# Linear attention and a soft mixture of experts on one core: joined early loads, a split weight load, and a first output chunk whose odd rows are stored in uneven pieces

## The chip, the core and the metric

The kernel runs on one core of one Trainium2 chip. A core has a tensor engine (PE, with its weight loads PEld), a vector engine (DVE), a scalar engine (ACT), GpSimd (POOL) and SyncE (SP), which work in parallel and wait for one another on semaphores, and sixteen DMA engines that move data between the chip's memory (DRAM) and the core's SBUF. The metric is the device time of one execution in microseconds. The profile is one more execution, recorded; its span runs from the first to the last recorded instruction.

## What is computed

The reference makes linear attention over 64 heads, joins the heads to 4608 tokens of 512 numbers, and sends the tokens through a soft mixture of 8 experts. All numbers are float32.

```python
def _attn_ref(q, k, v, g_norm):
    kv = np.einsum('bhsd,bhse->bhde', k, v)
    out = np.einsum('bhsd,bhde->bhse', q, kv)
    rms = np.sqrt(np.mean(out * out, axis=-1, keepdims=True) + 1e-06)
    return (out / rms * g_norm).astype(np.float32)

def _moe_ref(x, phi, w1, w2):
    logits = x @ phi
    d = np.exp(logits - logits.max(0, keepdims=True))
    d /= d.sum(0, keepdims=True) + 1e-09
    slot_input = (d.T @ x).reshape(E, S_per_e, D)
    for e in range(E):
        slot_out[e] = np.maximum(slot_input[e] @ w1[e], 0.0) @ w2[e]
    c = np.exp(logits - logits.max(1, keepdims=True))
    c /= c.sum(1, keepdims=True) + 1e-09
    return (c @ slot_out.reshape(n_slots, D)).astype(np.float32)
```

Here q, k and v are 8 x 8 x 576 x 64, phi is 512 x 32 (8 experts of 4 slots), each w1 is 512 x 1024 and each w2 is 1024 x 512. Inputs and result together are 71 MB.

## The kernel before

**Memory.** Nearly all of SBUF is one buffer, `arena`, in blocks of 256 columns; `place(at, n)` is n columns from block `at`. `KV_AT` and `Q_AT` say where the keys and values of each of the 8 batches (`kv`) and the queries of each pair of batches (`q`) lie, `W_AT` where the weights go that later overwrite them, `OUT_AT` where the 12 chunks of the result are put. A load or a store is one DMA instruction of 128 rows, one for each partition of SBUF, so that each of the sixteen DMA engines has 8 rows of it.

**Loads.** All DMAs are issued by SP, one after the other, each when its place is free. The first eight stand ahead of everything: `first` (constants and the first half of the first kv block), the second half of that block, the main part of the first q block, the second kv block in two halves, the rest of the first q block, the third kv block, the main part of the second q block. Three more follow once the first kv block is used up. The others wait for a tile of the main loop (`loads_behind`): the last kv and q blocks at tile 9, weights at tiles 18, 24 and 27. `W_ROWS` lists which weights share a load: its fourth row holds half of w2 of expert unit 2, w1 of expert 6 and w1 of expert 5, and is loaded after the last tile.

**Main loop.** 36 tiles of 128 tokens, T = 0 to 35. For each tile PE multiplies queries with a block-diagonal matrix `bd` made from k and v (`products`), ACT squares and copies the result out of PSUM (`square`, `evict`), DVE sums squares and logits, POOL scales rows (`scale_x`, `scale_part`). The matrix of a batch b is made in three steps: step 0 and step 1 multiply keys with values, step 2 (`slots`) transposes and fills `bd`. `kv_steps` says after which tile's turn a step stands: entry (b, i) is i tiles from the batch's first tile, `first[b]` = 9 * (b // 2) + 4 * (b % 2). A step stands ahead of `products` of its tile.

**Experts and output.** After the loop come the sums over the slots, `expert_h` (first matrix), `expert_y` (second matrix, in two halves hf of the result's columns), then `gather` and `mix`, and `output(hf, k, f)` for each of the 12 chunks: n = 0 to 5 for the first half, 6 to 11 for the second. A chunk is 1536 columns of `arena`. `OUT_ROWS` says which chunks go out in one store: chunks 0 to 2, 3 to 5, 6 and 7, 8 to 11; the store is issued once the last chunk of its row stands in `arena`. Between the chunks PE still multiplies for the second half: `expert_y(2, 1)` to `expert_y(5, 1)` after chunk 3, `expert_y(6, 1)` and `expert_y(7, 1)` after chunk 5. Their weights come with the last two loads (`load_w("w2", 5)`, `load_w("w2", 7)`).

**Order and waits.** The class `Order` records every instruction and derives the waits from what is read and written. All instructions therefore carry the line of its `emit`, L204 before and L208 after. At the end SP waits for those DMAs that nobody else waited for.

Of the kernel before, what the change touches and what calls it, by code (L numbers as in the profile page):

```python
# [5 lines left out]
F32 = mybir.dt.float32  # L6
# [5 lines left out]
P = 128  # L12
# [15 lines left out]
TOK = 4608  # L28
# [4 lines left out]
KV_AT = (0, 36, 54, 0, 90, 126, 18, 54)  # L33
Q_AT = (18, 72, 108, 36)
# [8 lines left out]
    (("w1", 4, None), ("w2", 2, 1), ("w2", 0, None), ("w2", 1, None)),  # L43
    (("w2", 2, 0), ("w1", 6, None), ("w1", 5, None)),
    (("w1", 7, None),),
# [4 lines left out]
OUT_AT = (32, 38, 44, 104, 110, 116, 122, 128, 134, 140, 146, 152)  # L50
OUT_ROWS = ((0, 1, 2), (3, 4, 5), (6, 7), (8, 9, 10, 11))
SHARED = (5, 11)
HEAD = 144
# [210 lines left out]

def soft_moe_linear_attention(nc, first_in, kv_in, q0_in, q1_in, kv4_in, kv5_in, t3_in, w_in, out):


    const = Const(nc)
# [12 lines left out]
    def load_row(at, src):  # L281
        nc.sync.dma_start(place(at, src.shape[-1]), src)
# [30 lines left out]
    def w_block(kind, u, i):  # L313
# [6 lines left out]
    nc.sync.dma_start(arena[:, : HEAD + 2304], first_in)  # L320
    load_row(KV_AT[0] + 9, kv_in[0, :, 2304:])
    load_row(Q_AT[0], q0_in[:, :2048])
    load_row(KV_AT[1], kv_in[1, :, :2304])
    load_row(KV_AT[1] + 9, kv_in[1, :, 2304:])
    load_row(Q_AT[0] + 8, q0_in[:, 2048:])
    load_row(KV_AT[2], kv_in[2])
    load_row(Q_AT[1], q1_in)

# [4 lines left out]
        24: lambda: load_w("w1", 2),  # L333
        27: lambda: load_w("w1", 4),
    }

# [6 lines left out]
    zeros = const.tile([P, 256], BF16, name="zeros")  # L343
    nc.vector.memset(zeros, 0.0)
    eps = const.tile([P, 1], F32, name="eps")
    nc.gpsimd.memset(eps, EPS_RMS)
# [6 lines left out]
    for i in range(2):  # L353
        lo = 64 * i
# [268 lines left out]
    first = {b: 9 * (b // 2) + 4 * (b % 2) for b in range(B)}  # L623
    kvs = {}
    kv_steps = {(b, i - 3): (i,) for b in range(2, B) for i in range(3)}
    kv_steps.update({(1, -2): (0,), (1, -1): (1, 2)})
    kv_steps.update({(6, i - 4): (i,) for i in range(3)})
# [49 lines left out]
    for g in range(2):  # L677
# [6 lines left out]
        fill(EARLY[1 + g], cols=512)  # L684
    load_row(KV_AT[3], kv_in[3])
    load_row(Q_AT[1] + 8, kv4_in)
    load_row(Q_AT[2], kv5_in)
    T_at, diag_at, pb_at, d_at, sums_at = {}, {}, {}, {}, {}
    for T in range(NT - 2):
# [3 lines left out]
        o = products(T)  # L693
# [182 lines left out]
    def mix(hf):  # L876
# [3 lines left out]
        zs[hf] = halves(f"z{hf}", pz)  # L880

    def output(hf, k, f):
        z = zs[hf]
# [4 lines left out]
        for v in range(2):  # L888
# [21 lines left out]
            else:  # L910
                nc.vector.tensor_copy(out=st[:, 2:4], in_=pots[0][:, :, : CT * NS])
        for row in OUT_ROWS:
            if row[-1] == n:
                lo, m = row[0] * 4 * CT * NS, len(row) * 4 * CT * NS
                nc.sync.dma_start(
                    out[:, lo * P : (lo + m) * P].rearrange("o (p n) -> (o p) n", p=P), place(OUT_AT[row[0]], m)
                )

    expert_h(0)
    expert_h(1)  # L920
# [42 lines left out]
def build_program():  # L963
    import concourse.bacc as bacc

    nc = bacc.Bacc("TRN2", target_bir_lowering=False, num_devices=1, dynamic_dma_scratch_size=SCRATCH)
    shapes = {
        "first": (P, HEAD + 2304), "kv": (4, P, TOK), "q0": (P, TOK), "q1": (P, 2048),
        "kv4": (P, 2560 + TOK), "kv5": (P, 2 * TOK), "t3": (P, 3 * TOK),
        "w": (1, 2 * NE * P * UNIT),  # L970
    }
    args = [nc.dram_tensor(f"in_{n}_dram", s, F32, kind="ExternalInput").ap() for n, s in shapes.items()]
    args.append(nc.dram_tensor("out_0_dram", (1, 4 * NCH * P * 4 * CT * NS), F32, kind="ExternalOutput").ap())
    order = Order(nc)
    soft_moe_linear_attention(order, *args)
    order.emit()
    return nc
# [58 lines left out]
```

## Time and profile before

| | us |
|---|---|
| median of 3 runs (172.42 to 172.51) | 172.49 |
| the profiled execution | 172.53 |
| its span | 171.2 |
| PE busy (87% of the span) | 149.1 |
| ACT busy (52%) | 88.9 |
| DVE busy (50%) | 86.0 |
| POOL busy (33%) | 57.2 |

DMA engines moved 71.67 MB in 3476 packets, 419 GB/s on the mean over the span. Matmuls overlap one another, so PE's share is not a measure of its reserve. A wait is read from the idle time just ahead of an instruction and from what ended it. A DMA is seen at three points: when SP issues it, when its rows are moved, and when the last of them has landed.

### The profile page before, as it was taken

The page shows a single profiled execution, that of the slowest core. Times are in us where ns is not written, and L with a number is a line of the kernel's source. Part 1 is how long each engine was busy: PE and PEld are TensorE (multiplying, and loading weights), DVE is VectorE, ACT ScalarE, POOL GpSimd, SP SyncE. Part 2 cuts the span into 40 slices and gives each one's busy share as a digit, 9 for nine tenths or more (in the row PEclk, how much of TensorE's full clock was granted, in tenths as well). Part 3 has the DMA queues.
Part 4 walks back from the last instruction along what each step waited for, and adds up shares of the span by engine and source line. Part 5 has one row for each costly group of instructions (what it writes and reads, how often), then busy time and mean ns, then how long its engine had stood idle before and what let it go on. Part 6 is the DMA issues. An engine that isn't in the chain of part 4 may idle for free.

```text
span 171.2 us, 4497 instructions
## 1 busy us (share of the span) xinstructions
PE 149.1 (87%) x1975; PEld 108.1 (63%) x1975; DVE 86.0 (50%) x184; ACT 88.9 (52%) x230; POOL 57.2 (33%) x68
## 2 busy tenths in 40 slices
PE   7787897989999899999899999999999988989400
PEld 3467776979688888898797775455565444445100
DVE  1122156283677265763936798724897027137400
ACT  2037576786965887768849864203213025137400
POOL 6000708548356755466482579200000000000000
PEclk9999999999999999999999999999999999999965
DMA  5999999999999999999999999998999999999995
GB/s 192 416 422 433 439 415 437 472 421 474 417 413 458 430 426 430 406 404 452 433 492 419 431 429 389 434 450 354 436 478 387 461 390 421 439 396 439 406 459 241
DMA packets 3476, 71.67 MB, mean 419 GB/s; under 512 B 384, under 2 KB 384, under 8 KB 384
## 3 DMA queue, kind: packets, MB, share of 16 engines
q1 hardware_dynamic: 3456, 71.38, 97.6%
q8 instruction: 15, 0.25, 0.5%
q14 instruction: 5, 0.04, 0.1%
HBM read 61.94 MB, written 9.44 MB: 417 GB/s over the span
## 4 chain that ended last, share of the span: by engine, by line
PE 47%; DMA 26%; ACT 12%; DVE 5%; SPq 2%; issue 1%
PE psum L204 47%; DMA arena<-in_kv_dram 13%; DMA arena<-in_w_dram 13%; ACT bd L204 3%; ACT sq L204 3%; ACT xall L204 2%; SPq L204 2%; DVE logits L204 1%; ACT arena L204 1%; DVE ms L204 1%; ACT part L204 1%; ACT d L204 1%; ACT r L204 1%; DVE r L204 0%; DVE d L204 0%
## 5 line engine op out<-in xcount | busy, mean ns | idle before, releaser
L204 PE MATMUL psum<-bd,arena 128*128 128x192 f32 (+1 forms) x320 | 56.1, 335 | 1.9 <-ACT bd L204 1.5
L204 PEld LDWEIGHTS psum<-bd,arena 128*128 128x128 f32 (+1 forms) x320 | 45.4, 179 | 7.1 <-ACT bd L204 2.8
L204 DVE TENSOR_REDUCE ms<-sq 128x16 f32<-128x1024 f32 (+1 forms) x19 | 22.1, 1162 | 32.6 <-ACT sq L204 32.3
L204 POOL TENSOR_TENSOR xall<-xall,r 128x512 f32<-128x512 f32 x34 | 34.8, 1044 | 0.0
L204 POOL TENSOR_TENSOR part<-part,r 128x512 f32<-128x512 f32 x17 | 17.8, 1049 | 49.7 <-DVE r L204 49.7
L204 ACT ACTIVATE sq<-psum 128x512 f32<-128x512 f32 x36 | 21.5, 598 | 12.6 <-PE psum L204 12.4
L204 PE MATMUL psum<-arena 128*64 128x64 f32 (+1 forms) x640 | 21.7, 226 | 3.3 <-DMA arena<-in_kv_dram 2.2
L204 PEld LDWEIGHTS psum<-arena 128*64 128x64 f32 (+1 forms) x640 | 19.0, 137 | 7.9 <-DMA arena<-in_kv_dram 3.5
L204 ACT COPY xall<-psum 128x512 f32<-128x512 f32 x34 | 20.6, 606 | 0.0
L204 ACT COPY part<-psum 128x256 f32<-128x256 f32 (+1 forms) x38 | 13.6, 359 | 9.9 <-DVE part L204 8.8
L204 DVE TENSOR_REDUCE logits<-part 128x64 f32<-128x512 f32 (+1 forms) x18 | 17.8, 991 | 0.0
L204 PE MATMUL psum<-arena,xall 128*32 128x256 f32 x256 | 15.0, 380 | 0.4 <-DMA arena<-in_w_dram 0.2
L204 DVE COPY arena<-psum 128x768 f32<-128x768 f32 (+1 forms) x12 | 10.4, 889 | 8.4 <-PE psum L204 8.4
L204 ACT COPY arena<-psum 128x768 f32<-128x768 f32 (+1 forms) x14 | 10.1, 755 | 8.3 <-PE psum L204 8.3
L204 PE MATMUL psum<-logits,part 32*128 32x384 f32 x96 | 12.8, 521 | 1.5 <-ACT arena L204 0.9
L204 PE MATMUL psum<-arena,sq 128*32 128x256 f32 x224 | 12.7, 379 | 0.2 <-DVE sq L204 0.2
L204 PEld LDWEIGHTS psum<-arena,xall 128*32 128x32 f32 x256 | 8.0, 110 | 7.3 <-DMA arena<-in_w_dram 1.8
L204 PE MATMUL psum<-xall,d 128*32 128x129 f32 x288 | 10.8, 278 | 0.9 <-ACT d L204 0.9
L204 ACT COPY bd<-psum 64x128 f32<-64x128 f32 (+1 forms) x32 | 9.9, 309 | 1.6 <-PE psum L204 1.4
L204 PEld LDWEIGHTS psum<-logits,part 32*128 32x128 f32 x96 | 6.1, 183 | 7.1 <-ACT arena L204 4.2
L204 PEld LDWEIGHTS psum<-arena,sq 128*32 128x32 f32 x224 | 7.2, 110 | 5.2 <-DVE sq L204 0.6
L204 PEld LDWEIGHTS psum<-xall,d 128*32 128x32 f32 x288 | 7.0, 109 | 4.1 <-ACT d L204 2.2
(74 smaller groups left out, 118.9 us busy)
## 6 DMA issues: line engine op xcount, KB each, us to landing
arena<-in_w_dram SPq DMA_DIRECT2D x4, 4096.0 KB, 19.9
arena<-in_w_dram SPq DMA_DIRECT2D x1, 7168.0 KB, 27.5
arena<-in_t_dram SPq DMA_DIRECT2D x1, 6912.0 KB, 36.1
arena<-in_w_dram SPq DMA_DIRECT2D x1, 5120.0 KB, 17.9
arena<-in_kv_dram SPq DMA_DIRECT2D x2, 2304.0 KB, 23.4
arena<-in_kv_dram SPq DMA_DIRECT2D x1, 4608.0 KB, 42.6
out_dram<-arena SPq DMA_DIRECT2D x2, 2304.0 KB, 9.6
arena<-in_kv_dram SPq DMA_DIRECT2D x1, 3584.0 KB, 32.2
```

Of the source, the lines that this page charges most:

```text
L204: inst = getattr(engine, method)(*args, **kwargs)
```

## The change

There are four edits.

1. **Joined early loads.** The second half of the first kv block and the main part of the first q block become one load, `kq0` (4352 columns); the two halves of the second kv block become one, `kv1`; the third kv block and the main part of the second q block become one, `kq2` (6656 columns). Eight early loads become five.
2. **Order of kv steps.** Batch 1 has steps 0, 1 and 2 all ahead of tile 3 (before: step 0 ahead of tile 2, steps 1 and 2 ahead of tile 3). Batch 2 has steps 0 and 1 ahead of tile 7 and step 2 ahead of tile 8 (before: one step each ahead of tiles 6, 7 and 8).
3. **Split w1 load.** w1 of expert 5 leaves its row of `W_ROWS` and is loaded behind tile 30; half of w2 unit 2 and w1 of expert 6 stay where the whole row was.
4. **First store.** Chunks 0 to 2 are no longer stored by one DMA of 128 rows. As soon as chunk 0 is there, its 64 odd rows (6,144 bytes each) go out in four pieces, `APART`: 26 rows as 2 x 13 from POOL, 11 rows as 2 x 11 half rows from POOL, 15 rows as 5 x 3 and 12 rows as 3 x 4 from SP. Once chunk 2 is there, the even rows of all three chunks (64 rows of 18,432 bytes) and the odd rows of chunks 1 and 2 (64 rows of 12,288 bytes) go out from SP. Two small loads on POOL into a new tile `steps`, with 7 and 6 outer pieces, stand ahead of POOL's first and second store. The host puts the pieces back in order.

```diff
     (("w1", 4, None), ("w2", 2, 1), ("w2", 0, None), ("w2", 1, None)),
-    (("w2", 2, 0), ("w1", 6, None), ("w1", 5, None)),
+    (("w1", 5, None),),
+    (("w2", 2, 0), ("w1", 6, None)),
...
+CHUNK = 4 * 12 * 32
+APART = (("gpsimd", 0, 26, 2, 1), ("gpsimd", 41, 11, 2, 2), ("sync", 26, 15, 5, 1), ("sync", 52, 12, 3, 1))
+STEPS = (7, 6)
...
-    load_row(KV_AT[0] + 9, kv_in[0, :, 2304:])
-    load_row(Q_AT[0], q0_in[:, :2048])
-    load_row(KV_AT[1], kv_in[1, :, :2304])
-    load_row(KV_AT[1] + 9, kv_in[1, :, 2304:])
-    load_row(Q_AT[0] + 8, q0_in[:, 2048:])
-    load_row(KV_AT[2], kv_in[2])
-    load_row(Q_AT[1], q1_in)
+    load_row(KV_AT[0] + 9, kq0_in)
+    load_row(KV_AT[1], kv1_in)
+    load_row(Q_AT[0] + 8, q0_in)
+    load_row(KV_AT[2], kq2_in)
...
         27: lambda: load_w("w1", 4),
+        30: lambda: load_w("w1", 5),
...
-    kv_steps.update({(1, -2): (0,), (1, -1): (1, 2)})
+    kv_steps.update({(1, -1): (0, 1, 2)})
+    kv_steps.update({(2, -2): (0, 1), (2, -1): (2,)})
+    del kv_steps[2, -3]
...
+    def step_over(n):
+        ends = [x[:n, : 2 * w].rearrange("p (c n) -> p c n", c=2)[:, :, :4] for x, w in ((steps, 8), (first_in, 64))]
+        nc.gpsimd.dma_start(*ends)
+
+    def store_apart():
+        at = 0
+        for j, (engine, lo, n, a, c) in enumerate(APART):
+            src = place(OUT_AT[0], CHUNK)[2 * lo + 1 : 2 * (lo + n) : 2]
+            size = n * CHUNK
+            dst = out[:, at : at + size].rearrange("o (b a n) -> (o a) b n", a=a, n=CHUNK // c)
+            if c > 1:
+                src = src.rearrange("p (c n) -> p c n", c=c)
+            getattr(nc, engine).dma_start(dst, src)
+            at += size
+            if j == 0:
+                step_over(STEPS[1])
+
+    def store_first():
+        at = 64 * CHUNK
+        for i in range(2):
+            n = (3 - i) * CHUNK
+            nc.sync.dma_start(out[:, at : at + 64 * n].rearrange("o (m n) -> (o m) n", n=n), place(OUT_AT[i], n)[i::2])
+            at += 64 * n
...
-        for row in OUT_ROWS:
+        if n == 0:
+            store_apart()
+        if n == 2:
+            store_first()
+        for row in OUT_ROWS[1:]:
...
+    step_over(STEPS[0])
     expert_h(0)
```

How this moves the instructions. PE, early part, before: 64x64 products of keys and values (`psum<-arena`), transposes (`ident,kvT`, `gphi,kvT`), and four 128x192 products for each tile (`bd,arena`).

```order
L204 MATMUL psum<-bd,arena 128x192 x8
L204 MATMUL psum<-arena 64x64 x16
L204 MATMUL psum<-bd,arena 128x192 x4
L204 MATMUL psum<-arena 64x64 x24
L204 MATMUL psum<-ident,kvT 128x128 x2
L204 MATMUL psum<-gphi,kvT 128x128 x2
L204 MATMUL psum<-bd,arena 128x192 x4
L204 MATMUL psum<-bd,arena 64x192 x8
L204 MATMUL psum<-bd,arena 128x192 x4
L204 MATMUL psum<-arena 64x64 x16
L204 MATMUL psum<-bd,arena 128x192 x4
L204 MATMUL psum<-arena 64x64 x24
```

The same place of PE after the change.

```order
L208 MATMUL psum<-bd,arena 128x192 x12
L208 MATMUL psum<-arena 64x64 x40
L208 MATMUL psum<-ident,kvT 128x128 x2
L208 MATMUL psum<-gphi,kvT 128x128 x2
L208 MATMUL psum<-bd,arena 128x192 x4
L208 MATMUL psum<-bd,arena 64x192 x8
L208 MATMUL psum<-bd,arena 128x192 x8
L208 MATMUL psum<-arena 64x64 x40
L208 MATMUL psum<-bd,arena 128x192 x4
L208 MATMUL psum<-ident,kvT 128x128 x2
L208 MATMUL psum<-gphi,kvT 128x128 x2
```

The products of tile 2 now stand ahead of both steps of batch 1, and those of tile 6 ahead of both steps of batch 2; the 16 and 24 products of a batch stand together as 40.

SP at the end of the program, before: the last load and the four stores.

```order
L204 DMA arena<-in_w_dram 128x4096
L204 DMA out_dram<-arena 128x4608 x2
L204 DMA out_dram<-arena 128x3072
L204 DMA out_dram<-arena 128x6144
L220 ISA
```

SP at the end of the program after the change.

```order
L208 DMA arena<-in_w_dram 128x4096
L208 DMA out_dram<-arena 5x3x1536
L208 DMA out_dram<-arena 3x4x1536
L208 DMA out_dram<-arena 64x4608
L208 DMA out_dram<-arena 64x3072
L208 DMA out_dram<-arena 128x4608
L208 DMA out_dram<-arena 128x3072
L208 DMA out_dram<-arena 128x6144
L224 ISA
```

The first store of 128 rows has become two pieces of chunk 0 and two stores of 64 rows; the other three stores are as before.

POOL at the end of its program after the change; before, the clearing of `sq` was its last instruction.

```order
L208 TENSOR_TENSOR xall<-xall,r 128x4x128 x2
L208 MEMSET sq 128x1024
L208 DMA steps<-in_first_dram 7x2x4
L208 DMA out_dram<-arena 2x13x1536
L208 DMA steps<-in_first_dram 6x2x4
L208 DMA out_dram<-arena 2x11x768
```

Four DMAs have been put behind it, two of them small loads into `steps`.

## Rows read from the trace of the kernel before

**Rows 1.** Busy tenths in 40 equal slices: POOL, and the sixteen DMA engines.

```profile
POOL 6000708548356755466482579200000000000000
...
DMA  5999999999999999999999999998999999999995
```

**Rows 2.** Stretches: from:to, length, busy time of five engines, PEclk, DMA share, GB/s.

```profile
5.00:100.00 95.00, 88.51 (x1210) 75.22 (x1210) 50.85 (x108) 67.58 (x187) 46.99 (x47) 1.00 1.02 435
151.30:151.90 0.60, 0.60 (x20) 0.34 (x16) 0.10 (x1) 0.24 (x1) 0.00 (x0) 1.00 0.65 277
161.60:162.00 0.40, 0.00 (x0) 0.00 (x0) 0.00 (x0) 0.00 (x0) 0.00 (x0) 1.00 0.51 215
162.00:162.20 0.20, 0.00 (x0) 0.00 (x0) 0.00 (x0) 0.00 (x0) 0.00 (x0) 1.00 2.70 1167
162.20:163.00 0.80, 0.00 (x0) 0.00 (x0) 0.00 (x0) 0.00 (x0) 0.00 (x0) 1.00 1.13 476
168.30:169.10 0.80, 0.00 (x0) 0.00 (x0) 0.00 (x0) 0.00 (x0) 0.00 (x0) 0.50 1.14 492
169.10:169.90 0.80, 0.00 (x0) 0.00 (x0) 0.00 (x0) 0.00 (x0) 0.00 (x0) 0.50 0.51 215
```

**Rows 3.** SP's issues in order of time: start, length, instruction.

```profile
1.64 0.42 SPq L204 DMA_DIRECT2D arena<-in_q_dram  x1
...
4.30 0.72 SPq L204 DMA_DIRECT2D arena<-in_q_dram  x1
...
161.19 0.33 SPq L204 DMA_DIRECT2D out_dram<-arena  x1
```

**Rows 4.** The same three DMAs: size, and us from issue to landing.

```profile
arena<-in_q_dram SPq DMA_DIRECT2D x1, 1024.0 KB, 9.9
...
arena<-in_q_dram SPq DMA_DIRECT2D x1, 1024.0 KB, 24.8
...
out_dram<-arena SPq DMA_DIRECT2D x1, 3072.0 KB, 9.9
```

**Rows 5.** The chain that ended last, from 122: start, length, what.

```profile
122.21 22.24 DMA arena<-in_w_dram
...
159.61 0.96 PE psum L204 x4
```

**Rows 6.** PE from 134: start, length, instruction, idle time before and its releaser.

```profile
134.67 0.42 PE L204 MATMUL psum<-arena,xall 128*32 128x256 f32 x4 [0.25 <-DMA arena<-in_w_dram]
...
143.40 0.97 PE L204 MATMUL psum<-logits,part 32*128 32x384 f32 x8 [0.36 <-DVE arena L204]
...
144.49 0.42 PE L204 MATMUL psum<-arena,xall 128*32 128x256 f32 x4
```

**Rows 7.** Queue of instruction fetches: packets, MB, share of sixteen engines' span.

```profile
q8 instruction: 15, 0.25, 0.5%
```

**Rows 8.** PE from 9 to 36, early part: as in rows 6.

```profile
9.10 1.43 PE L204 MATMUL psum<-arena 128*64 128x64 f32 x40
...
15.61 1.15 PE L204 MATMUL psum<-arena 128*64 128x64 f32 x32 [0.88 <-DMA arena<-in_kv_dram]
...
26.70 1.15 PE L204 MATMUL psum<-arena 128*64 128x64 f32 x32 [1.28 <-DMA arena<-in_kv_dram]
27.78 1.57 PE L204 MATMUL psum<-bd,arena 128*128 128x192 f32 x8
29.28 1.54 PE L204 MATMUL psum<-arena 128*64 128x64 f32 x48
...
32.16 0.38 PE L204 MATMUL psum<-ident,kvT 128*128 128x128 f32 x2
```

**Rows 9.** Who waited for whom, PE's matmuls: us in total, times, longest.

```profile
PE psum L204 <- DMA arena<-in_kv_dram: 2.2, 2, 1.3
...
PE psum L204 <- DMA arena<-in_w_dram: 0.2, 1, 0.2
```

More of the change, by code (lines that the diff above doesn't have):

```diff
@@ L262, in row_length, with apart_pieces, soft_moe_linear_attention @@
     return sum(UNIT if part is None else UNIT // 2 for _, _, part in row)
-def soft_moe_linear_attention(nc, first_in, kv_in, q0_in, q1_in, kv4_in, kv5_in, t3_in, w_in, out):
+def apart_pieces():
+    return [
+        np.array([(2 * m + 1, h, c) for m in range(lo, lo + n) for h in range(c)]).reshape(a, -1, 3).swapaxes(0, 1).reshape(-1, 3)
+        for _, lo, n, a, c in APART
+    ]
+def soft_moe_linear_attention(nc, first_in, kq0_in, kv1_in, q0_in, kq2_in, kv3_in, kv4_in, kv5_in, t3_in, w_in, out):
     const = Const(nc)
@@ L344, in soft_moe_linear_attention @@
     nc.vector.memset(zeros, 0.0)
+    steps = const.tile([P, 16], F32, name="steps")
     eps = const.tile([P, 1], F32, name="eps")
@@ L684, in soft_moe_linear_attention @@
         fill(EARLY[1 + g], cols=512)
-    load_row(KV_AT[3], kv_in[3])
+    load_row(KV_AT[3], kv3_in)
     load_row(Q_AT[1] + 8, kv4_in)
@@ L967, in build_program @@
     shapes = {
-        "first": (P, HEAD + 2304), "kv": (4, P, TOK), "q0": (P, TOK), "q1": (P, 2048),
+        "first": (P, HEAD + 2304), "kq0": (P, 2304 + 2048), "kv1": (P, TOK), "q0": (P, 2560),
+        "kq2": (P, TOK + 2048), "kv3": (P, TOK),
         "kv4": (P, 2560 + TOK), "kv5": (P, 2 * TOK), "t3": (P, 3 * TOK),
@@ L1017 @@
         "in_first_dram": first,
-        "in_kv_dram": kv[:4],
-        "in_q0_dram": qm[0],
-        "in_q1_dram": np.ascontiguousarray(qm[1][:, :2048]),
+        "in_kq0_dram": np.concatenate([kv[0][:, 2304:], qm[0][:, :2048]], axis=1),
+        "in_kv1_dram": kv[1],
+        "in_q0_dram": np.ascontiguousarray(qm[0][:, 2048:]),
+        "in_kq2_dram": np.concatenate([kv[2], qm[1][:, :2048]], axis=1),
+        "in_kv3_dram": kv[3],
         "in_kv4_dram": np.concatenate([qm[1][:, 2048:], kv[4]], axis=1),
@@ L1029 @@
     n = 4 * CT * NS
-    chunks = []
-    for row in OUT_ROWS:
+    three = np.empty((P, 3 * n), np.float32)
+    at = 0
+    for pieces in apart_pieces():
+        for p, h, c in pieces:
+            w = n // c
+            three[p, h * w : h * w + w] = res[0, at : at + w]
+            at += w
+    three[::2] = res[0, at : at + 192 * n].reshape(64, 3 * n)
+    three[1::2, n:] = res[0, at + 192 * n : 3 * P * n].reshape(64, 2 * n)
+    chunks = [three[:, k * n : k * n + n] for k in range(3)]
+    for row in OUT_ROWS[1:]:
         part = res[0, row[0] * n * P : (row[-1] + 1) * n * P].reshape(P, len(row), n)
```

## The prediction, made before the result was known

> **What bounds the kernel now.** I read the page first, from the busy tenths down. The line of the DMA engines is at 9 from the second slice to the last but one, once at 8 [rows 1], and no other engine is so full for so long: the program streams 71 MB, and sixteen DMA engines set the pace. In the long steady stretch they move 435 GB/s [rows 2], 27.2 GB/s each. So the next question was where DMA engines stand still, and the table of stretches answers it (a row of a transfer counts there in the stretch in which it begins, so bytes divided by the row length give the number of rows begun). At the end, 168.3 to 169.1 shows 492 GB/s x 0.8 us = 394 KB, 16 rows of 24,576 B, and 169.1 to 169.9 shows 172 KB, 7 rows [rows 2]. Sixteen engines, each with eight such rows: nine begin their last row in the first stretch, seven begin one more after it. A row takes 24,576 / 27.2 = 0.90 us, and the seven are late by about 1.15 us (the middle of the one group of last rows to that of the other). The same split shows where the last store begins: from 162.0 to 162.2 the table counts 233 KB, nine rows of 24,576 B and one of 12,288 B, after 161.6 to 162.0 with a share of 0.51 [rows 2]. Nine engines stood ready and began together some 0.9 us after SP issued that store at 161.19 [rows 3]; seven were still busy with the store before. The last store lands at 161.19 + 9.9 = 171.1 [rows 3, 4], which is the end of the span of 171.2.
>
> So two things end this program almost together: seven late engines that never rest, and for the nine others the time at which the last store is issued. That time hangs on the tensor engine (PE). The chain of waits has the landing of the second last weight load, 122.21 + 22.24 = 144.45, and from there matmuls and copies to the end [rows 5]. Ten microseconds before it PE waits 0.25 us for the first of the late weight loads at 134.67, and its outputs in between end at 143.40 + 0.97 = 144.37, 0.12 before its next start at 144.49 [rows 6]: from 134 on PE has about 0.37 us in hand, no more.
>
> Why seven are late no row says outright. The queue of instruction fetches has 15 packets that cost 0.5% of 16 engines' span, 13.7 us or 0.9 us each [rows 7]; fetches that fall on some engines twice and on others never would do it.
>
> **The odd rows of the first output chunk: less for some engines.** Before, one store of chunks 0 to 2 with 128 rows gives each engine eight rows of 18,432 B. Now the 64 odd rows of chunk 0 (6,144 B each, 0.226 us at 27.2 GB/s) are taken out and stored by four transfers with 2, 2, 5 and 3 outer pieces; the rest stays even. An engine that gets none of them saves four rows, 0.90 us; one that gets 13 has nine more, 2.03 us. If the seven late engines are among those with none, they end at 171.1 - 0.9 = 170.2. If they are not, they end as before or up to 2.03 later. These are the bounds, and no row names the engine of a packet. I take the first, because the lag repeats: three timed runs agree within 0.09 us, so the same engines can be late each time, and the shapes take from many engines (64 rows on at most twelve) to load few.
>
> The Trainium skill, "DMA: Bandwidth & Descriptors", section "Why a DMA increments its semaphore by 16 and not by 1", says that the outer counts of both sides set the number of engines, from the lowest engine for SP and from a rotating cursor for GpSimd (POOL). By it eight engines get none, three get 7, two get 3, two get 13 and one 11. No run here shows it; with it the sum stays the one above.
>
> The loaded engines must not become the new last ones. Five of the nine have most in hand: from 151.3 to 151.9 the share is 0.65 [rows 2], so about five or six engines stood still, waiting for the second store. Their lead over the seven is the 1.15 us at the end, about 0.75 us of this standstill (some 3.8 engine-us over five) and half of 0.4 us again from 161.6 to 162.0 at a share of 0.51: 2.1 to 2.6 us. Against 2.03 us more work they end 0.1 to 0.6 us before the old end, 170.5 to 171.0; the two with the longest lead belong to the upper part, so 170.5.
>
> The price in issues: POOL gets two small loads into `steps` and two stores. It has no work from slice 27 on (tenths at 0) [rows 1], so nothing is queued behind them. No POOL transfer is in the trace; SP's issues, 0.33 to 0.72 us each [rows 3], put two stores near 1 us, and at ten times that they would still be out before the end. SP issues two more after the first chunk and two instead of one where the old store stood: three more at 0.33, about 1 us, in front of the store of chunks 3 to 5, which has to wait for chunk 5 anyway. All of it lies in SP's waits.
>
> **The joined early loads.** Three fewer transfers move the same bytes. Since the steady share is 1.02 [rows 2], there is no gap between transfers to win back: 0, at most 0.1 us. What they do is land later. The second half of the first key/value block was awaited alone and now comes with the q block behind it, at 1.64 + 9.9 = 11.5 [rows 3, 4] where PE began at 9.10 [rows 8]: 2.4 us later. The third key/value block now lands with the next q block at 4.30 + 24.8 = 29.1 [rows 3, 4] where PE began on it at 26.70 [rows 8]: again 2.4. PE gives part of this back: its waits of 0.88 at 15.61 and 1.28 at 26.70 [rows 8] vanish, and the new order puts the products of tile 6 (1.50, from 27.78 to 29.28) ahead of the wait. From 26.70 to the transposes at 32.16 PE took 5.46; without those products it needs 3.96, from 29.1 on: 33.1, or 0.9 us late. Bounds: 0, if the rest is caught too, and 2.4, if nothing is. After that nothing catches it until 134.67: the table of waits has two waits of PE's matmuls for the early loads, 2.2 us in all, which are these two, and one of 0.2 us for a weight load, which is the one at 134.67 [rows 9]. So 0.9 arrives there, 0.37 is caught by the slack of [rows 6], and the last store is issued 0.5 us later (bounds 0 and 2.03).
>
> The clock: PE now stands still from about 9.0 to 11.5. In the trace its last matmul ends at 159.61 + 0.96 = 160.6 [rows 5], and up to 163.0 the granted clock is still 1.00, the upper of its two levels (2.4 GHz) [rows 2]. I price this at nothing.
>
> **The split w1 load.** The weights of expert 5 get their own load after tile 30, the rest stays where it was and comes 0.9 later. It adds one issue to a waiting SP. It costs nothing and it covers the late start: 2 MB more in the queue is 4.8 us of stream.
>
> **The sum, against the profiled execution (172.53 us, span 171.2).** Late engines: 170.2. Nine others: they end now at 171.1 - 1.15 = 169.95, plus 0.5 for the later issue, 170.45. Loaded engines: 170.5. The last of these is 170.5, 0.6 us less than 171.1: time 171.9. The median of the three runs is 0.04 below the profiled run, which changes nothing at this precision: **171.9 us**. With each bound: 171.5 if the late start is wholly caught, 172.4 if the loaded engines come in at their late end.
>
> **Rivals.** *The late start eats it.* If the delay of PE reaches the last store with more than 1.15 us, all nine engines end after the old end and nothing is gained; that is so from a delay of 1.5 us at tile 8 on. For it: the chain from 35 to 134 has no wait for data that could catch anything. Against it: the two waits and the moved products. Time 172.2 to 173.4, most of it near 172.5. *The extra rows go to late engines (slower).* The store with two outer pieces puts 13 rows on each of two engines. If one of these is among the seven, it ends 2.03 us after 171.1, and the time is 174.5; it decides as soon as its lead is under 2.03 us. For it: no row says which engines are late. The Trainium skill, "DMA: Bandwidth & Descriptors", section "Latency and other measured facts", has engines 7 and 15 as usually slower than the others; by that rule and the one above, the loaded engines would be the slow ones. The trace neither confirms nor denies it, since it shows a lag of seven engines, not of two. *The shares come out even after all*, the pieces spread over a dozen engines: the late ones lose two rows instead of four, 0.45 us, and the time is 172.1.
>
> **How the numbers follow.** Forecast 0.62, late start 0.16, rows on late engines 0.13, even shares 0.09. A difference under 0.2% (0.35 us) can't be told from none. Faster: nearly all of the first and half of the last, 0.64. Same: the late start mostly, and the other half, 0.20. Slower: 0.16. The range goes from 171.4 (late start caught, a little from fewer transfers) to 172.9, which leaves out the case of 174.5 and the far end of the late start.
>
> **What would show it.** In the table of stretches the last 1.5 us should have all sixteen last rows close together, not nine and then seven. The last store should be issued 0.3 to 0.8 us later than 161.19. PE should wait near 9 to 11.5 for the joined load and reach the transposes for the third block near 33.1; with 34 or later, the first rival is true. The share at 151.3 to 151.9 should be higher than 0.65. A lone engine busy well after the others at the end would be the second rival.

## The result, and the profile after

The changed kernel takes 173.99 us (median of six runs, 173.55 to 174.59) against 172.49: a ratio of 1.0087 [1.0075, 1.0099]. It is 1.5 us slower where 0.6 us faster was forecast, and above the range. The profiled execution took 173.87 us, its span is 172.6.

The page shows first what the prediction priced at nothing. These are its busy tenths of the granted clock and of the DMA engines (40 slices of 4.3 us), which answer [rows 1], and the shares of the chain that ended last.

```profile
PEclk9987999999999999999999999999999999999965
DMA  5999999999999998999999997999999999999994
...
PE 64%; ACT 15%; DVE 7%; DMA 6%; issue 1%; SPq 0%
```

The clock is down in the third and fourth slice; before, it was at 1.00 from 5 to 100 us [rows 2]. The chain has only one DMA piece to speak of, the load of `kq0`; from its landing on, PE and the engines that work for it lead to the end. Before, the chain had a weight load of 22 us in it [rows 5].

PE's early part after the change, to be laid beside [rows 8]: start, length, instruction, idle time before and its releaser.

```profile
11.33 2.35 PE L208 MATMUL psum<-arena 128*64 128x64 f32 x40 [2.55 <-DMA arena<-in_kq_dram]
...
28.59 1.57 PE L208 MATMUL psum<-bd,arena 128*128 128x192 f32 x8 [0.76 <-ACT xall L208]
30.09 2.48 PE L208 MATMUL psum<-arena 128*64 128x64 f32 x80
...
33.90 0.38 PE L208 MATMUL psum<-ident,kvT 128*128 128x128 f32 x2
...
36.68 1.57 PE L208 MATMUL psum<-bd,arena 128*128 128x192 f32 x8 [0.65 <-ACT bd L208]
```

The first products of tile 9 before, which [rows 8] does not show:

```profile
34.94 1.57 PE L204 MATMUL psum<-bd,arena 128*128 128x192 f32 x8 [0.65 <-ACT bd L204]
```

PE starts on `kq0` at 11.33 instead of 9.10, after 2.55 us of standing still, and the same 40 products take 2.35 us instead of 1.43 [rows 8]. At the third kv block it waits for no load at all; what it waits for just ahead of it is ACT, which copies an earlier tile out of PSUM into `xall`. The transposes come at 33.90 instead of 32.16, 1.74 us late, and tile 9 starts at 36.68 instead of 34.94, with the same 1.74.

Stretches of the same trace (from:to, length, busy time of PE, PEld, DVE, ACT, POOL, then PEclk, DMA share, GB/s; a row counts where it begins).

```profile
11.40:14.80 3.40, 3.40 (x44) 2.69 (x44) 0.00 (x0) 0.48 (x2) 0.00 (x0) 0.50 1.01 434
14.80:30.00 15.20, 13.62 (x151) 11.61 (x150) 5.72 (x12) 10.70 (x29) 4.80 (x5) 1.00 1.01 431
...
161.80:165.00 3.20, 0.00 (x0) 0.00 (x0) 0.52 (x1) 0.48 (x1) 0.00 (x0) 1.00 0.96 407
...
169.35:170.25 0.90, 0.00 (x0) 0.00 (x0) 0.00 (x0) 0.00 (x0) 0.00 (x0) 0.50 1.01 437
170.25:172.25 2.00, 0.00 (x0) 0.00 (x0) 0.00 (x0) 0.00 (x0) 0.00 (x0) 0.50 0.09 37
...
169.60:170.40 0.80, 0.00 (x0) 0.00 (x0) 0.00 (x0) 0.00 (x0) 0.00 (x0) 0.50 1.14 492
170.40:171.20 0.80, 0.00 (x0) 0.00 (x0) 0.00 (x0) 0.00 (x0) 0.00 (x0) 0.50 0.08 31
```

From 11.4 to 14.8 the clock is at its lower level, 1.2 GHz. At the end, 437 GB/s x 0.90 us is 393 KB, sixteen rows of 24,576 B, and after 170.25 three more rows begin (37 x 2.00 = 74 KB). Divided otherwise, sixteen rows begin from 169.6 to 170.4 (492 x 0.80 = 394 KB) and one after it (31 x 0.80 = 25 KB). Before, seven engines were one row behind [rows 2]; now fifteen are within a row of one another, as the prediction wanted to see, and one alone runs on.

SP's issues and POOL's DMAs (start, length), and three rows on size and time from issue to landing, which answer [rows 3, 4].

```profile
76.56 27.88 SPq L208 DMA_DIRECT2D arena<-in_w_dram  x4
...
162.40 0.33 SPq L208 DMA_DIRECT2D out_dram<-arena  x1
```

```profile
143.48 0.63 POOL L208 DMA_DIRECT2D out_dram<-arena  x1 [33.01 <-ACT arena L208]
144.10 0.58 POOL L208 DMA_DIRECT2D steps<-in_first_dram  x1
144.68 0.83 POOL L208 DMA_DIRECT2D out_dram<-arena  x1
```

```profile
arena<-in_kq_dram SPq DMA_DIRECT2D x1, 3328.0 KB, 26.3
...
out_dram<-arena SPq DMA_DIRECT2D x1, 3072.0 KB, 10.0
arena<-in_kq_dram SPq DMA_DIRECT2D x1, 2176.0 KB, 10.1
```

The last store is issued 1.21 late, at 162.40 instead of 161.19, and lands 10.0 later, at 172.4. POOL's issues cost 0.6 to 0.8 us each and stand in idle time, as the prediction had it.

### The profile page after: what moved, and what is told of

It reads as the page before. It is cut to its first block, busy times and chain, and to the rows that moved or that the text cites. A ratio compares the mean times of both kernels' runs of the same rounds, so it can differ in the third digit from the quotient of the medians.

```text
span 172.6 us, 4507 instructions
## 1 busy us (share of the span) xinstructions
PE 150.4 (87%) x1975; PEld 109.2 (63%) x1975; DVE 85.9 (50%) x184; ACT 88.6 (51%) x230; POOL 59.9 (35%) x72
## 4 chain that ended last, share of the span: by engine, by line
PE 64%; ACT 15%; DVE 7%; DMA 6%; issue 1%; SPq 0%
PE psum L208 64%; DMA arena<-in_kq_dram 6%; ACT sq L208 4%; ACT bd L208 4%; ACT xall L208 3%; DVE ms L208 2%; ACT arena L208 2%; DVE logits L208 1%; ACT part L208 1%; ACT r L208 1%; DVE arena L208 1%; ACT d L208 1%; DVE part L208 1%; DVE r L208 0%; DVE d L208 0%
## 5 line engine op out<-in xcount | busy, mean ns | idle before, releaser
L208 PE MATMUL psum<-arena 128*64 128x64 f32 (+1 forms) x640 | 22.2, 232 | 3.0 <-DMA arena<-in_kq_dram 2.6
L208 PEld LDWEIGHTS psum<-arena 128*64 128x64 f32 (+1 forms) x640 | 19.7, 142 | 7.0 <-DMA arena<-in_kq_dram 2.9
L208 POOL DMA_DIRECT2D out_dram<-arena x2 | 1.5, 728 | 33.0 <-ACT arena L208 33.0
```

Source lines behind the costliest of these rows:

```text
L208: inst = getattr(engine, method)(*args, **kwargs)
```

## The experiments

Sixteen kernels. Those of one group (e1 to e4, e5 to e8, e9 to e12, e13 to e16) ran on the same chip and share the runs of the kernel before (medians 172.60, 172.54, 172.61, 172.62), so ratios are compared across groups. The theory, called L below, was: the joined loads (edits 1 and 2 together) are the whole loss, by the clock and by PE's late start; the store is a small gain. The rivals put it on the uneven store, on the larger transfers as such, or on the clock alone.

### Which edit loses

e1 is the kernel before with edits 1 and 2 alone, e2 with edit 4 alone, e3 with edits 3 and 4, e12 with edit 3 alone.

```diff
 e1
-    load_row(KV_AT[0] + 9, kv_in[0, :, 2304:])
-    load_row(Q_AT[0], q0_in[:, :2048])
+    load_row(KV_AT[0] + 9, kq0_in)
...
+    kv_steps.update({(2, -2): (0, 1), (2, -1): (2,)})
 e2, e3
+        if n == 0:
+            store_apart()
 e3, e12
+        30: lambda: load_w("w1", 5),
```

> The kernel before with the joined early loads and the new order of kv steps alone; first store and w1 row as before. Theory L (the joined loads make PE late, and PE sets when the last store is issued): PE stands still about 2.5 us near 9 to 11.3, the granted clock falls to 1.2 GHz after it, tile 9 begins at 36.5 to 36.8 and the last store is issued at 162.2 to 162.5 as in the changed kernel. With the even first store the seven late engines still end near 171.1, so the time is 172.5 to 173.2. Theory S (the uneven store does the harm: its pieces load an engine that is late): no change here, 172.4 to 172.6, whatever PE does.

> The kernel before with the first store in uneven pieces alone; loads as before. Theory L: the last store is issued at 161.2 as before, the late engines save up to four rows (0.9 us), time 171.5 to 172.0. Theory S: the loss is here, 173.4 to 174.2, with an engine alone at the end.

> The changed kernel with the early loads and the kv steps put back as they were: uneven first store and split w1 load alone. Theory L: 171.4 to 172.0, the last store issued at 161.1 to 161.3. Theory S: 173.4 to 174.2. If the split w1 load does something by itself, this differs from the uneven store alone by more than 0.3 us.

> The kernel before with the split w1 load alone (w1 of expert 5 behind tile 30). The prediction put this edit at nothing: 172.4 to 172.6. Rival: the earlier issue keeps the queue full near 110 us, where the uneven-store kernels with and without it differ by 0.1 us (172.35 and 172.44): 172.3 to 172.45.

| | us, median | ratio to before |
|---|---|---|
| e1, joined loads | 174.55 (173.03 to 175.59) | 1.0098 [1.0062, 1.0135] |
| e2, uneven store | 172.44 (172.08 to 173.81) | 1.0003 [0.9986, 1.0021] |
| e3, uneven store and split load | 172.35 (171.92 to 172.86) | 0.9986 [0.9976, 0.9996] |
| e12, split load | 172.70 (172.46 to 172.80) | 1.0000 [0.9991, 1.0009] |

The whole loss is in edits 1 and 2, the joined loads with their order of kv steps, and comes even larger without the other edits; my expectation for e1 was too low. No kernel has one of these two edits without the other, so what the new order does by itself is not shown. e3 is the fastest kernel here that stores everything, a little faster than before, but e2 and e3 both miss what I expected of them (at most 172.0). Stretches of e1, early:

```profile
9.00:11.70 2.70, 0.45 (x14) 0.45 (x16) 0.00 (x0) 0.00 (x0) 0.00 (x0) 1.00 0.99 425
11.70:18.50 6.80, 6.61 (x49) 5.73 (x45) 0.44 (x2) 1.54 (x6) 0.00 (x0) 0.50 0.99 421
```

In this run the lower clock held for 6.8 us, twice as long as in the changed kernel. The spread of e1's six runs goes with the mean granted clock: 0.953 to 0.967 at 174.5 to 175.6 us, 0.976 and 0.977 at 173.8 and 173.0.

The gain of the store is small: e2's interval includes no change at all, e3's does not. The end of e2 and of e3, in stretches:

```profile
169.35:170.25 0.90, 0.00 (x0) 0.00 (x0) 0.00 (x0) 0.00 (x0) 0.00 (x0) 0.50 0.20 82
```

```profile
169.35:170.25 0.90, 0.00 (x0) 0.00 (x0) 0.00 (x0) 0.00 (x0) 0.00 (x0) 0.50 0.07 27
```

And the same stretch of the kernel before:

```profile
169.35:170.25 0.90, 0.00 (x0) 0.00 (x0) 0.00 (x0) 0.00 (x0) 0.00 (x0) 0.50 0.38 164
```

After 169.35 three rows begin in e2 (82 x 0.90 = 74 KB) and one in e3, where before it was six (148 KB). So most of the late engines are brought forward, and one to three engines still end late.

### The clock

e4 is the changed kernel with ten instead of one of the dummy matmuls that PE runs after the first half of batch 0, to fill its wait for `kq0`; e5 is e1 with the same.

```diff
-EARLY = (5, 1, 0)
+EARLY = (5, 10, 0)
```

> The changed kernel with ten fill matmuls instead of one behind the first half block (nine more, without use for the result), so that PE does not stand still before the joined load lands. Theory L with the clock as its larger part: the granted clock stays at 1.00, tile 9 begins near 35.8 instead of 36.7, the last store is issued near 161.6 instead of 162.4, time 173.0 to 173.3. If the clock is no part of it: 173.8 to 174.2. Theory S: no change from the changed kernel, 173.5 to 174.5.

> The kernel before with the joined early loads and the new order of the kv steps (even first store, unsplit w1 row), and with more of the early matmuls that only keep PE busy while it waits for kq0, so that the granted clock should stay at 1.00 (2.4 GHz) from 5 us on. Theory L (the join costs twice: once through the clock, once because PE reaches tile 9 about 0.85 us late, which holds back the weight load behind tile 24 and lets the queue run dry): the late start alone is left, tile 9 near 35.8 instead of 34.94, last store issued near 161.7 to 162.0, time 172.9 to 173.3. Rival C (the clock is the whole loss): 172.4 to 172.6. Rival B (the larger transfers themselves are slower, whatever PE does): 174.0 or more, as in the kernel with the joined loads and the clock drop (174.55).

e4: 173.09 (172.33 to 173.77), ratio 1.0024 [1.0008, 1.0039]. e5: 173.00 (172.44 to 173.53), 1.0022 [1.0008, 1.0035]. So filling the wait with useless work won back 0.9 us in the changed kernel and 1.5 in e1; by the ratios, since these kernels ran beside different runs of the kernel before, it is 1.1 and 1.3. PE of e4, one stretch of it, and its last store:

```profile
11.39 1.43 PE L208 MATMUL psum<-arena 128*64 128x64 f32 x40 [0.59 <-DMA arena<-in_kq_dram]
...
29.18 2.48 PE L208 MATMUL psum<-arena 128*64 128x64 f32 x80
...
32.99 0.38 PE L208 MATMUL psum<-ident,kvT 128*128 128x128 f32 x2
...
35.77 1.57 PE L208 MATMUL psum<-bd,arena 128*128 128x192 f32 x8 [0.65 <-ACT bd L208]
```

```profile
11.40:14.80 3.40, 2.94 (x48) 2.32 (x49) 0.44 (x2) 0.79 (x3) 0.00 (x0) 1.00 0.98 423
...
169.35:170.25 0.90, 0.00 (x0) 0.00 (x0) 0.00 (x0) 0.00 (x0) 0.00 (x0) 0.50 0.26 109
170.25:172.25 2.00, 0.00 (x0) 0.00 (x0) 0.00 (x0) 0.00 (x0) 0.00 (x0) 0.50 0.06 25
```

```profile
161.56 0.33 SPq L208 DMA_DIRECT2D out_dram<-arena  x1
```

The start is as late as in the changed kernel (11.39), but the 40 products take 1.43 again, the clock stays at 1.00, and tile 9 is 0.83 late instead of 1.74. So the larger transfers as such are not the greater part of the loss. 0.5 us to before is left, so the clock is not all of it, and of this rest the larger transfers could still be a part. The last store is only 0.37 late here, yet after 169.35 still six rows begin, two of them after 170.25. This profiled run, at 173.57, is one of the slower of e4's twelve.

The changed kernel's own runs point the same way. Five of its six have a mean clock of 0.960 to 0.968 and take 173.87 to 174.59; the sixth has 0.976, within the 0.970 to 0.982 of e2 to e5, which have no early wait of that length, and takes 173.55. Only the profiled run has a trace, so that the clock held in the sixth is inferred.

### The late start

e7 is e4 with w1 of expert 2 loaded behind tile 20 and only that of expert 3 behind tile 24. e9 is the changed kernel without the join in `kq2`, e10 without the join in `kq0`.

```diff
 e7
-    (("w1", 2, None), ("w1", 3, None)),
+    (("w1", 2, None),),
+    (("w1", 3, None),),
...
-        24: lambda: load_w("w1", 2),
+        20: lambda: load_w("w1", 2),
+        24: lambda: load_w("w1", 3),
 e9
-    load_row(KV_AT[2], kq2_in)
+    load_row(KV_AT[2], kq2_in[:, :TOK])
+    load_row(Q_AT[1], kq2_in[:, TOK:])
 e10
-    load_row(KV_AT[0] + 9, kq0_in)
+    load_row(KV_AT[0] + 9, kq0_in[:, :2304])
+    load_row(Q_AT[0], kq0_in[:, 2304:])
```

> The changed kernel with PE kept busy during its wait for kq0 (173.09 without the next edit), and with w1 of expert 2 loaded behind tile 20 and w1 of expert 3 behind tile 24 instead of both behind tile 24. Theory Q (with PE 0.83 us late, the load behind tile 24 is issued too late for the fast engines, the queue runs dry and they lose their lead): the dip near 77 to 78 us goes, the engines with 13 rows end 0.5 to 1 us earlier, time 172.4 to 172.7. Rival P (the late start reaches the end through PE and the issue of the last store alone, 161.56): 173.0 to 173.2 as before.

> The changed kernel with the third kv block and the main part of the second q block in two loads again, as before; kq0 and kv1 stay joined, the new order of the kv steps too. Theory K0 (kq0 alone makes PE late and drops the clock; when PE comes to the third kv block at 30.09, its load has long landed): nothing is won back, tile 9 near 36.6 to 36.7, time 173.7 to 174.2. Rival K2 (the wait for the third kv block in the joined load is a good part of the loss): tile 9 before 36.2, time 173.4 or less.

> The changed kernel with the second half of the first kv block and the main part of the first q block in two loads again, as before; kq2 and kv1 stay joined, the new order of the kv steps too. PE should begin on the first block near 9.1, so the granted clock stays at 1.00. Theory K0 as far as the clock goes: 0.9 us or more is won back against the changed kernel (173.99). Then the two theories on the late start part: by the working of the prediction the wait for kq2 alone (landing near 29) makes PE 0.7 to 0.9 late at tile 9, so tile 9 near 35.6 to 35.8 and a time of 172.8 to 173.2; if kq2 is hidden behind the products of tile 6, tile 9 is near 34.9 to 35.2 and the time 172.2 to 172.5.

e7: 172.65 (172.28 to 173.88), 1.0010 [0.9994, 1.0026]. The load behind tile 24 is issued at 76.56 after the change, at 74.82 before. GB/s from 70 to 90 in the trace of the changed kernel, of e4 and of e7:

```profile
70.00:90.00 20.00, 19.42 (x304) 16.79 (x303) 12.82 (x27) 15.03 (x43) 11.71 (x13) 1.00 1.01 421
```

```profile
70.00:90.00 20.00, 19.41 (x299) 16.94 (x289) 12.54 (x26) 14.70 (x42) 11.72 (x12) 1.00 1.02 428
```

```profile
70.00:90.00 20.00, 19.43 (x293) 17.11 (x291) 12.43 (x26) 14.46 (x41) 11.72 (x13) 1.00 1.02 438
```

The kernel before has 438 there too. That would fit a queue left short by a load that comes late, but it does not show it. e4's load behind tile 24 is issued at 75.68; e5, e9 and e10 also have both w1 loads there, issued at 75.53, 75.42 and 75.55, and show 441, 437 and 440. And 17 GB/s over 20 us are 340 KB, six rows of the 57,344 B that begin near the end of this stretch: whether a few of them begin just before 90 or just after makes the difference. In time, e7 gains 0.44 us on e4 between the medians and 0.24 by the ratios, and the intervals overlap: it is not settled. The dip at 77 to 78 that I expected to vanish did not (328 GB/s in e4, 295 in e7), though a stretch of 1 us holds too few rows to judge by.

In e5 the late start arrives whole, and the last store is issued 0.92 late:

```profile
162.11 0.33 SPq L204 DMA_DIRECT2D out_dram<-arena  x1
```

e5 does without the split w1 load, and here the split shows its worth. In e10, which has it, PE is equally late at tile 9 (35.66 in both), but at the first late weights e5 waits for a load and e10 does not. PE of e5, then of e10:

```profile
135.75 3.66 PE L204 MATMUL psum<-arena,xall 128*32 128x256 f32 x64 [0.62 <-DMA arena<-in_w_dram]
```

```profile
135.08 3.66 PE L208 MATMUL psum<-arena,xall 128*32 128x256 f32 x64
```

e10's last store goes out at 161.41, 0.22 late. (This is one trace of each, and they differ in `kq0` and in the first store too.) In e4, e7, e9 and e10, which all have the split load, tile 9 is 0.59 to 0.83 late and the last store 0.07 to 0.37: 0.46 to 0.52 of the delay is caught on the way, where the prediction had 0.37.

e9: 174.19 (172.89 to 174.34), 1.0073 [1.0046, 1.0099]. e10: 173.08 (172.71 to 174.86), 1.0045 [1.0022, 1.0068]. Taking `kq2` apart wins nothing back; taking `kq0` apart wins 0.9. PE of e10, and then PE and a stretch of e9's profiled run:

```profile
29.07 2.48 PE L208 MATMUL psum<-arena 128*64 128x64 f32 x80 [0.41 <-DMA arena<-in_kq_dram]
...
35.66 1.57 PE L208 MATMUL psum<-bd,arena 128*128 128x192 f32 x8 [0.65 <-ACT bd L208]
```

```profile
11.26 1.43 PE L208 MATMUL psum<-arena 128*64 128x64 f32 x40 [1.96 <-DMA arena<-in_kq_dram]
...
35.53 1.57 PE L208 MATMUL psum<-bd,arena 128*128 128x192 f32 x8 [0.65 <-ACT bd L208]
```

```profile
11.40:14.80 3.40, 2.94 (x49) 2.32 (x48) 0.45 (x2) 0.79 (x3) 0.00 (x0) 1.00 1.01 434
```

Without the join in `kq0` tile 9 is 0.72 late (e10), and what PE waits for last is the load that the prediction named, landing at 29.07 where 29.1 was forecast. The wait itself is only 0.41: `kv1`, for which PE waits 1.99 up to 18.17, and the 0.76 for ACT at the moved products would have made tile 9 about 0.3 late without it. Without the join in `kq2` tile 9 is 0.59 late (e9), by the start and by ACT. `kv1` stays joined in both, and no run takes it apart. In e9's profiled run PE stood still for 1.96 us instead of 2.55, the clock stayed up, and the run took 172.89 us, where the three others took 174.12 to 174.34 at mean clocks of 0.966 to 0.972; that the clock fell in those three is inferred, since they have no trace, and 0.972 alone would not tell. Of e10's ten runs three show a lower mean clock (0.959 to 0.969) and take 173.77 to 174.86; the seven others take 172.71 to 173.16.

### The uneven store

e8 is e3 with other small loads ahead of POOL's stores; e6 is e3 with 8 instead of 13 rows on the pair and 5 instead of 3 on the five; e11 is e3 with SP's 15 rows as 3 x 5. e13 to e16 are e3 without one piece each. Pair, eleven, fives and threes are the four pieces of `APART`: 2 x 13 rows and 11 rows from POOL, 5 x 3 and 3 x 4 from SP.

```diff
 e8
-STEPS = (7, 6)
+STEPS = (9, 4)
 e6
-APART = (("gpsimd", 0, 26, 2, 1), ("gpsimd", 41, 11, 2, 2), ("sync", 26, 15, 5, 1), ("sync", 52, 12, 3, 1))
+APART = (("gpsimd", 0, 16, 2, 1), ("gpsimd", 41, 11, 2, 2), ("sync", 16, 25, 5, 1), ("sync", 52, 12, 3, 1))
 e11
-("sync", 26, 15, 5, 1)
+("sync", 26, 15, 3, 1)
 e13, with j = 0; e14 to e16 with 1 to 3
-            getattr(nc, engine).dma_start(dst, src)
+            if j != 0:
+                getattr(nc, engine).dma_start(dst, src)
```

> The split w1 load and the uneven first store, early loads as before, with 9 and 4 outer pieces in the two small loads into steps instead of 7 and 6. If the place of POOL's transfers goes by the pieces issued before them, the 13 rows fall on two other engines, and the 11 half rows stay where they were. Theory W (the shares are placed, and the engines now hit are late ones): last landings near 172.5 to 173.3, time 173.8 to 174.6. Rival N (the steps place nothing): 172.2 to 172.5, as with 7 and 6 (172.35).

> The split w1 load and the uneven first store, early loads as before, and the odd rows shared out otherwise: the two engines with 13 rows get 8, the five rows-of-five transfers carry 25 rows instead of 15. Theory T (the two engines with 13 rows end last, about 0.4 to 0.7 us behind the formerly late ones, and eat the gain): they have 5 rows of 0.226 us less, 1.1 us, so the last landings are at the ends of the formerly late engines, 170.1 to 170.4, and the time is 171.6 to 171.9. Rival G (the end is set by the issue of the last store and the engines behind it, the pair makes no difference): 172.2 to 172.5, as with 13 rows (172.35).

> The split w1 load and the uneven first store, early loads as before, with SP's first piece of 15 odd rows in 3 outer pieces of 5 rows instead of 5 of 3. If an SP store goes to as many engines as it has outer pieces, from the same first engine on, two engines are freed of 3 rows (0.68 us) and three have 9 instead of 7. Theory F (the lone last engine of the uneven store is a late one that has the 3 rows): last landings 170.1 to 170.5, time 171.7 to 172.0. Rival M (the last one is among the three that have most from SP, or is none of the five): 172.3 to 172.8.

> The split w1 load and the uneven first store, early loads as before (172.35), with one piece of the odd rows left out: the 26 rows of the transfer with two outer pieces are not stored. If the engines that carry these rows (13 each) are the last ones, as the prediction's sum had it, the time falls to 171.7 to 172.0, where the formerly late engines end; if others are last, it stays within 172.2 to 172.5.

> The same kernel with another piece left out: the 11 rows of POOL's second store are not stored. 171.7 to 172.0 if the engine or engines that carry them are the last ones, 172.2 to 172.5 if not.

> The same kernel with another piece left out: the 15 rows of SP's store with five outer pieces of three are not stored, 0.68 us less for five engines. 171.7 to 172.0 if these are the last ones (the kernel in which the rows go out as 3 x 5 lost 0.86 us, which speaks for it), 172.2 to 172.5 if not.

> The same kernel with another piece left out: the 12 rows of SP's store with three outer pieces of four are not stored, 0.90 us less for three engines. 171.7 to 172.0 if these are the last ones, 172.2 to 172.5 if not.

| | us, median | ratio to before |
|---|---|---|
| e3, for comparison | 172.35 | 0.9986 [0.9976, 0.9996] |
| e8, pair moved | 174.67 (174.61 to 174.74) | 1.0119 [1.0102, 1.0136] |
| e6, pair lighter | 172.51 (171.96 to 173.17) | 0.9996 [0.9982, 1.0010] |
| e11, 15 rows on three | 173.21 (172.47 to 174.01) | 1.0025 [1.0002, 1.0048] |
| e13, without the pair's rows | 174.15 (174.12 to 174.34) | 1.0088 [1.0075, 1.0102] |
| e14, without the eleven | 172.21 (171.79 to 172.55) | 0.9975 [0.9965, 0.9985] |
| e15, without the fives | 172.40 (171.98 to 172.87) | 0.9985 [0.9975, 0.9996] |
| e16, without the threes | 172.31 (171.85 to 172.67) | 0.9980 [0.9971, 0.9990] |

The end of e8, and of e13:

```profile
169.35:170.25 0.90, 0.00 (x0) 0.00 (x0) 0.00 (x0) 0.00 (x0) 0.00 (x0) 0.50 0.20 82
170.25:172.25 2.00, 0.00 (x0) 0.00 (x0) 0.00 (x0) 0.00 (x0) 0.00 (x0) 0.50 0.09 37
```

```profile
169.35:170.25 0.90, 0.00 (x0) 0.00 (x0) 0.00 (x0) 0.00 (x0) 0.00 (x0) 0.50 0.07 27
170.25:172.25 2.00, 0.00 (x0) 0.00 (x0) 0.00 (x0) 0.00 (x0) 0.00 (x0) 0.50 0.06 25
```

e8 shows that shares are placed: two more pieces ahead of POOL's first store, with the second store left where it was, cost 2.3 us. e13 shows it against my expectation. With fewer bytes to store it is 1.8 us slower, and its end has one row after 169.35 and two after 170.25: one engine, some three rows of 0.9 us behind the rest. Eleven rows of 6,144 B are 2.5 us by the prediction's 0.226 each. The best reading is that POOL's second store has come two places earlier, and that its rows now lie on a late engine. The Trainium skill, "DMA: Bandwidth & Descriptors", section "Why a DMA increments its semaphore by 16 and not by 1", has a POOL transfer on fewer than sixteen engines go to consecutive engines from a round-robin cursor. e8 and e13 agree with it, though no row names an engine.

My theory for e6 (the pair alone is last) missed, and so did the one for e11. Leaving out any one of the other three groups gives 0.2 us at most. e11 lost 0.86 us (0.7 by the ratios) where three engines got two rows more, 0.45 us; and by the count of its expectation e6 has three engines with nine rows too and lost at most 0.2. So the count does not explain e11, and its loss stays open.

The trace keeps start, length, size and queue of every row, though no view prints them. In each run sixteen rows of 24,576 B are followed by no further one; they are the engines' last. They end at:

| | us from the start of the span |
|---|---|
| before | nine at 169.32 to 169.47, one at 170.13, six at 170.52 to 170.68 |
| e3 | five at 169.37 to 169.43, ten at 169.78 to 170.07, one at 170.49 |
| e13 | nine at 169.34 to 169.47, six at 169.84 to 169.97, one at 172.32 |
| e9 | fourteen at 169.39 to 169.93, one at 170.70, one at 171.07 |
| e4 | fourteen at 169.69 to 170.56, one at 171.21, one at 171.70 |
| changed kernel | thirteen at 170.53 to 170.92, two at 171.21 and 171.26, one at 172.03 |

On a busy engine a row begins 3 to 4 ns before the one ahead of it ends, so the last engine can be followed back by the times, with some doubt where two engines' rows coincide. In e13 it has eleven of the odd rows, all from POOL, as worked out above. In the changed kernel it has thirteen: it is one of the pair, and ends 0.77 us after the next engine. In e3 it has none of the odd rows and ends 0.42 after the next: followed back over 30 us, it never rests. That fits with no group of odd rows winning much when it is left out or made lighter.

## Why the prediction was wrong, step by step

The sum said 171.9; the changed kernel took 173.99. By the ratios, times 172.49, the missing 2.1 us are three terms: e3 lies 0.35 above the forecast, e4 another 0.66 above e3, and the changed kernel 1.09 above e4. (By the medians, of different groups, they are 0.45, 0.74 and 0.90.)

**What bounds the kernel** was right: the late engines, and for the others the time at which the last store is issued. That store came 1.21 late, and where nine engines ended near 169.4 before, thirteen now end at 170.53 to 170.92. Taking four rows from the late engines (term 170.2, 0.9 less) worked in the main: in e13 six engines end at 169.84 to 169.97, where six ended 0.7 later before. But in e3 one engine without odd rows ends at 170.49, hardly earlier than the latest before, and no run says why.

**The clock: the step that failed most.** "I price this at nothing" rested on a row from the end of the program, where the clock stays at 1.00 after the last matmul. That row is true, after the change too: from 161.8 to 165.0 PE does nothing and has 1.00. But there more than 150 us of work lie behind, and near 9 us only eight; whether that is what differs, no run tests. The trace of before had no idle stretch of that length there, so the price had to be bounded by the nearest rows instead: the 40 products twice as long are 1.4 us more [rows 8], and all that follows until the clock is back comes on top. Measured: 0.9 us at tile 9 (35.77 in e4 against 36.68), 0.84 at the last store (161.56 against 162.40), 0.9 to 1.1 in time.

**The late start: its size right in part by luck, its price wrong.** Without the clock, tile 9 is 0.83 late and the last store 0.37; forecast were 0.9 and 0.5. The landing of `kq2` was forecast well, and e10 goes the way of the prediction. But the sum let the 0.9 pass through `kq2` alone, and in e4 PE comes to the third kv block with nothing to wait for: there it is the start at 11.4, 2.29 late, of which the two vanished waits give back 2.16, and a new wait of 0.76 for ACT at the moved products, which the prediction did not have. That this comes to the same size is luck.

The price was to be paid by the nine other engines alone. But the odd rows can't go out before chunk 0 stands, so the loaded engines begin late as well: POOL's first store is issued at 142.28 in e3, 142.64 in e4 and 143.48 in the changed kernel. And the engines lose lead in some way that PE does not show: in e9's profiled run the odd rows go out 0.06 later than in e3 and the last store 0.02 later, yet its last engine ends 0.58 later. Whether the load behind tile 24 or the larger transfers do this is open. This is the 0.66 us between e3 and e4, of which 0.32 is the later issue of the last store.

**The loaded engines: the term that was mis-sized.** 170.5 was the middle between guesses on the lead, 2.1 to 2.6 us, summed from shares of stretches shorter than a row (its 3.8 engine-us are 3.4 by the row itself), and had no late start in it. With early loads as before, no loaded engine ends behind the lone late one (e3). In the changed kernel an engine of the pair ends alone, 0.77 us after all others. Its thirteen rows took 4.4 us there, as the times of the rows tell, where the sum had 13 x 0.226 = 2.9: seven of POOL's 37 rows took over 0.3 us, the longest 0.68, and none did in e2 and e4, where the mean was 0.234. Why these seven took longer is not shown. The gain of the store is 0 to 0.25 us (e2, e3) instead of 0.6.

**The rivals.** The first, the late start eats the gain, came true, at a PE delay of 1.74 where it put its point at 1.5; its time of 172.2 to 173.4 was too low for want of the clock. Of the second, the lone engine at the end is there (0.77 us), but it is a loaded engine whose lead ran out, with the others issued late too. Thirteen rows on an engine without lead is what e8 looks like, at 174.67 against the 174.5 that the prediction gave for it. **The split load** cost nothing (e12), as forecast, and covered part of the late start, as forecast too (e10 against e5). The issues on SP and POOL stayed hidden. The share at 151.3 to 151.9 rose, as forecast, from 0.65 to 0.87.

## What to carry to other kernels

When a change makes PE wait early in a program, read the granted clock of that stretch as unknown, not as what it is elsewhere, and price the work behind the wait at both levels; a filler of a few dummy matmuls tells in one run which it is. Carry a delay into every term of the sum that waits for the delayed tiles: here the pieces of the first store waited for them as well as the last store did. Shares that differ by engine pay only while each engine's lead is known to within a row, in the program as it will be after the change.

## What the runs showed of the hardware that was not expected

- PE idle for 2.55 us near 9 us dropped the clock to 1.2 GHz for 3.4 us in the changed kernel and 6.8 in e1; idle for 1.96 us in e9's profiled run did not. At the end of the program PE kept 2.4 GHz through 3.2 idle us. By their times and mean clocks, the same kernel lost its clock in some runs and not in others, 0.6 us or more apart (e9, e10).
- Leaving out a store made the kernel 1.8 us slower (e13): the next store's eleven rows then lay on one engine that ended 2.35 us after all others.
- Unequal shares widen the spread of a kernel's times: e3 0.9 us and e6 1.2 us over twelve runs, where the split load with even shares (e12) had 0.3 over eleven.
